# Edits to the hand-written order of an attention and MLP kernel: group 6's transposes, group 9's load, a part of each weight matrix, and two copies moved to VectorE

## The chip, the cores and the metric

The kernel runs on one core of a Trainium2 chip. The metric is the device time of one execution in microseconds (us). It is given as the median of several runs. One execution more was recorded by the hardware profiler, and all durations and instants below come from that one, counted from the start of its span.

Five engines work side by side, each through its own list of instructions in order: TensorE (PE, matmuls), VectorE (DVE), ScalarE (ACT), GpSimd (POOL) and SyncE (SP). Semaphores hold an instruction back until what it reads is there and what it overwrites is no longer needed. An instruction that waits holds back everything behind it on its engine.

## What is computed

Eight batches of twelve attention heads (448 positions, head size 64) with normalized queries and keys, and behind it an MLP over all 3584 tokens.

```python
def rmsnorm(x, g):
    rms = np.sqrt(np.mean(x * x, axis=-1, keepdims=True) + 1e-06)
    return x / rms * g
q_n, k_n = (rmsnorm(q, g_q), rmsnorm(k, g_k))
scores = scale * np.matmul(q_n, k_n.transpose(0, 1, 3, 2))
attn = softmax(scores)
x = np.matmul(attn, v)        # then heads side by side: 3584 x 768
...
h = x @ w_in                  # 768 x 2048
g = np.maximum(h, 0.0) + alpha * np.minimum(h, 0.0)
return (g @ w_out)            # 2048 x 768, float32
```

## The kernel before

**Groups.** The twelve heads of a batch are done in three groups of four, so there are 24 groups y = 0 to 23; groups 0, 1, 2 are batch 0. For each group and each of q and k the steps are, in this order:

- `load_qk` (L97): two DMAs on SP's queue for q and two for k, into one of six `nat` buffers, which are three groups' worth. A buffer is free again when the group's scaling has read it.
- `square` (L141): on ScalarE for groups 0 and 1, on POOL for the others. `reduce` (L151): the sum over the head's 64 values, on VectorE. `root` (L159): two small ScalarE instructions that give 1 over the root mean square.
- `scale` (L168): the multiplication by that, to 16 bits, mostly on POOL; group 3's q is scaled on VectorE, its k on POOL.
- Turning: positions have to go to the free dimension. Up to group 5 this is 14 transposes on PE, and two VectorE copies out of PSUM (`turn`, L188). From group 6 on (`TD` = 6) it is two DMA transposes issued on SP (`turn_dma`, L178), which wait for the scaling, and later one VectorE multiplication of kT by the gain (`turn`, L191).
- `score` and `soft` (L225, L243): seven tiles per group; PE's matmuls, then ScalarE's exp. `den`, `log`, `invert`, `attv` (L269 to L312): the sum over keys, its reciprocal and the product with v, which leave `xT`.

**MLP.** `up(b, ft)` (L344) does one of 16 column blocks of w_in for batch b: six matmuls into a PSUM bank (`hT`), ScalarE's copy `ah` = alpha times h (L354), and VectorE's maximum of the two into `gT` (L355). `down(b0, t, oh)` (L357) multiplies 128 tokens with one half (oh) of w_out's columns, 16 matmuls, eviction by VectorE (L377), output by SP's queue. Of PSUM's banks, two (tag "mm") serve ups, downs and early transposes in turn, and a pair (tag "acc") serves denominators, products with v, and now and then a spare up (`hTa`) or down (`opa`). Batch 0's first four ups are begun early (`begin`, L335): ups 0 and 1 in the "mm" banks, 2 and 3 together in the "acc" pair, named `hTb`.

**Weights.** w_in is loaded in four parts of four column blocks (`load_w_in`, L119, three DMAs each), w_out in four quarters (`load_w_out`, L131): quarters 0 and 1 are the upper and lower half of the rows for oh 0, quarters 2 ("the third") and 3 ("the fourth") the same for oh 1. The issues stand on POOL's queue, among POOL's squares and scales.

**Order.** Everything is laid out in 69 bursts n. A planner (L402 to L562) spreads the score tiles over bursts and puts ups and downs into each burst's gap. Dictionaries hang the other steps on bursts: `prep` (start of a burst, by `at`), `post` (its end, by `after`), `roots` (root and the two scales of a group, just ahead of the gap, or in `late`, after so many ups of the gap), `jobs` (a reduce after each up, or a down's own list ahead of its eviction) and `turns`. `lead` is burst 10, in which batch 0's attention ends and its ups begin; there a reduce waits until `done` is at least 4, and root and scale come when `done` is 4.

The bursts around the change, with the start of their first score matmuls in the profile:

| burst | from, us | gap | hung on it |
|---|---|---|---|
| 5 | | | second part of w_in (post) |
| 7 | 27.6 | | root and scale 3; squares 4, third part of w_in (post) |
| 8 | 30.0 | | squares 5, fourth part (post) |
| 9 | 34.5 | | load 6 (prep); reduces 4 (post) |
| 10 (`lead`) | 37.3 | ups 0 to 4 | root and scale 4; reduces 5; w_out quarters 0 and 1, squares 6 (post) |
| 11 | 45.3 | ups 5, 6 | root and scale 5 |
| 12 | 50.1 | ups 7, 8 | turn 4; load 7, v of batch 1 (prep); quarter 2 (post) |
| 13 | 53.7 | ups 9 to 11 | reduces 6 |
| 14 | 58.1 | ups 12, 13 | root, scale and DMA transposes of 6; squares 7, quarter 3 (post) |
| 15 | 61.6 | ups 14, 15 | turn 5; load 8 (prep) |
| 16 | 65.3 | down (t 0, oh 0) | load 9 (prep); reduces 7 |
| 17 | 68.9 | down (1, 0) | root, scale, DMA transposes of 7; turn 6; squares 8 (post) |
| 18 | 73.9 | down (2, 0) | squares 9 (post) |
| 19 | 80.6 | down (0, 1) | load 10 (prep); reduces 8; turn 7 |
| 20 | 87.8 | down (1, 1) | v of batch 2 (prep); root, scale, DMA transposes of 8; reduces 9 |
| 21 | 92.5 | batch 1, ups 0 to 3 | root, scale, DMA transposes of 9 |
| 22 to 24 | 97.7 | ups 4 to 15 | turn 8 in burst 23 |

Down (0, 1) of burst 19 is the first reader of w_out's quarters 2 and 3: its first eight matmuls read quarter 2, its last eight quarter 3.

Of the kernel before, what the change touches and what calls it, by code (L numbers as in the profile page):

```python
# [12 lines left out]
ALU = mybir.AluOpType  # L13
# [8 lines left out]
def kernel(  # L22
# [12 lines left out]
    nc = tc.nc  # L35

    B, H, S, D = q.shape
# [4 lines left out]
    G = HH // 2  # L42
# [6 lines left out]
    TD = min(6, NG)  # L49
# [34 lines left out]
    alpha_sb = cols[:, :NF]  # L84
# [3 lines left out]
    gT = cst.tile([128, NF, W], FP16, name="gT", tag="gT")  # L88
# [226 lines left out]
    def bank(name, spare):  # L315
        if spare:
            t = psa.tile([128, 2, 512], FP32, name=name + "a", tag="acc")
            return t[:, 0]
        return psf.tile([128, 512], FP32, name=name, tag="mm")
# [3 lines left out]
    def up_part(hT, b, ft, lo, hi):  # L323

        for i in range(lo, hi):
            for g in range(2):
                nc.tensor.matmul(  # L327
                    out=hT[:, :S],
                    lhsT=w_in_sb[:, g * G + i, ts(ft, 128)],
                    rhs=xT[b][:, g, i, :],  # L330
                    start=(i == 0 and g == 0),
                    stop=(i == G - 1 and g == 1),
                )

    def begin(ft):  # L335
# [5 lines left out]
            begun[2], begun[3] = t[:, 0], t[:, 1]  # L341
        up_part(begun[ft], 0, ft, 0, G - 1)

    def up(b, ft, spare=False):  # L344
        if b == 0 and ft in begun:
            hT = begun[ft]

            for n in {2: (2, 3), 3: ()}.get(ft, (ft,)):
                up_part(begun[n], 0, n, G - 1, G)
        else:  # L350
            hT = bank("hT", spare)
            up_part(hT, b, ft, 0, G)
        ah = ffn.tile([128, S], FP16, name="ah", tag="ah", bufs=3)
        nc.scalar.activation(out=ah, in_=hT[:, :S], func=AF.Copy, scale=alpha_sb[:, ft : ft + 1])  # L354
        nc.vector.tensor_max(out=gT[:, ft, ds((b & 1) * S, S)], in0=hT[:, :S], in1=ah)  # L355

    def down(b0, t, oh, jobs=(), spare=False):  # L357

# [44 lines left out]
    den_at, av_at, split = {}, {}, {}  # L403
# [5 lines left out]
    while m < NG * J or steps:  # L409
        n = len(bursts)  # L410
        while steps:
# [14 lines left out]
        late = both or n in dens and n in avs or any(  # L426
            y >= G for y in dens.get(n, avs.get(n, ()))
        )
        limit = 2 + late + (both and avs[n][0] >= G)
        bursts.append([])  # L430
        while len(bursts[n]) < limit and m < NG * J:
            y, j = divmod(m, J)
# [11 lines left out]
    prep, post, roots = {}, {}, {}  # L444

    def at(n, f, *a):
        prep.setdefault(max(int(n), 0), []).append((f, a))

    def after(n, f, *a):
        post.setdefault(max(int(n), 0), []).append((f, a))  # L450

    turn_at = {
        y: max(n for n in range(first_in[y]) if y >= TD or n not in dens)
        for y in range(1, NG)
    }
    turn_at[2], turn_at[G] = 5, av_at[0]
    turn_at.update((y, den_at[y - 2]) for y in range(TD, NG) if y % G == 1)
    turns = {n: y for y, n in turn_at.items()}
    jobs = {}
    for y in range(G, NG):  # L460

        early = y < G + 2
        if early:
            n = turn_at[y - 1] + 1
        elif y == G + 2:
            n = den_at[G - 1]
        elif y == 2 * G:
            n = turn_at[y] - 4
        elif y % G == 1:
            n = den_at[y - 4] - 1  # L470
        elif y % G:
            n = den_at[y - G]
        else:
            n = av_at[y - 4]
        at(n - (6 if early else 4 if y <= 3 * G else 5), load_qk, y)
        for nm in "qk":
            if y != 2 * G:
                after(n - 2, square, y, nm)
            if early:
                after(n, reduce, y, nm)  # L480
            else:
                jobs.setdefault(n, []).append((reduce, (y, nm)))
        roots[n + 1] = y
    for b in range(1, B):
        at(av_at[G * b] - 6, load_v, b)

# [26 lines left out]
    first = av_at[G - 1]  # L513
# [54 lines left out]
    for n, g in enumerate((g_q, g_k)):  # L568
        for h in range(2):
            nc.gpsimd.dma_start(  # L570
                out=rows[NF + n : NF + n + 1, ds(64 * h, 64)], in_=g.unsqueeze(0)
# [13 lines left out]
    for nm in "qk":  # L585
# [3 lines left out]
        out=gain, in0=cols[:, NF : NF + 1], in1=cols[:, NF + 1 : NF + 2]  # L589
# [12 lines left out]
    after(0, load_w_in, 0)  # L602
    for nm in "qk":
        after(2, reduce, 2, nm)
    after(5, load_w_in, 1)
    after(7, load_w_in, 2)
    after(8, load_w_in, 3)
    for c in range(4):
        after(first + (0, 0, 2, 4)[c], load_w_out, c)
    for nm in "qk":  # L610
        after(first, square, 2 * G, nm)
    roots[3] = 2
# [2 lines left out]
    for n in range(NB):  # L615
        for f, a in prep.get(n, ()):
            f(*a)
        tiles = bursts[n]

        lead = n == den_at[G - 1]  # L620
        first_tiles = tiles[: 2 if lead else split.get(n, 2)]
        for t in first_tiles:
            score(*t)
            if n == den_at[G - 1] - 1 and t == tiles[-1]:
                begin(0)
                begin(1)
            elif lead and t == tiles[0]:
                soft(*t)
                den(dens[n])
                attv(avs[n], 0, True, (log, invert))  # L630
            elif lead and t == tiles[1]:
                begin(2)
        plain = lead or n not in dens and n not in avs
        wait = plain and not lead and gaps[n] and gaps[n][0][0] is up
        if lead:
            begin(3)
        for t in tiles[:1] if wait else tiles[1:2] if lead else first_tiles:
            soft(*t)
        if n in dens and not lead:
            den(dens[n])  # L640
        if n in avs and not lead:

            for half in (1, 0) if avs[n] == (0, 1) else (0,):
                attv(avs[n], half)
        for t in () if lead else tiles[len(first_tiles) : 3]:
            score(*t)
            soft(*t)
        if n in avs and len(avs[n]) == 2 and avs[n] != (0, 1):
            attv(avs[n], 1)
        for t in () if lead else tiles[max(len(first_tiles), 3) :]:  # L650
            score(*t)
            soft(*t)
        late = []
        if wait:
            late = [(1, soft, t) for t in tiles[1:]]
        if n in roots:
            y = roots[n]
            work = [(root, (y,)), (scale, (y, "q")), (scale, (y, "k"))]
            if lead:

                late = [(2, score, tiles[2]), (2, soft, tiles[2])]
            if lead or wait and y < TD:
                late += [(4 if lead else 1, f, a) for f, a in work]
            else:
                for f, a in work:
                    f(*a)
            if y >= TD:
                turn_dma(y)
        if n in dens and not lead:
            log(dens[n])  # L670
            if gaps[n] and gaps[n][0][0] is down:
                invert(dens[n])
            else:
                late = [(1, invert, (dens[n],))]
        done = 0

        spare_at, clock = [], 0.0
        taken = n + 1 in dens or n + 1 in avs or turns.get(n + 1, TD) < TD
        for k, (f, a) in enumerate(gaps[n]):
            free = 2.3 if n in dens else (0.1, 1.2, 0.0)[len(avs.get(n, ()))]  # L680
            since += 1
            if clock >= free and not turns.get(n, TD) < TD and (
                since > 2 and not (taken and k == len(gaps[n]) - 1) or free == 0.0 and k == 0
            ):
                spare_at.append(k)
                since = 0
            clock += DOWN if f is down else UP
        ups_first = gaps[n] and gaps[n][0][0] is up
        if ups_first and n in dens and not lead:
            for f, a in jobs.pop(n, ()):  # L690
                f(*a)
        turned = n in turns and gaps[n] and (turns[n] >= TD or turns[n] < 2 * G)
        if turned and not ups_first and turns[n] >= TD:
            jobs.setdefault(n, []).append((turn, (turns[n],)))
        elif turned:
            turn(turns[n])
        for k, (f, a) in enumerate(gaps[n]):
            spare = k in spare_at
            if f is down:
                down(*a, jobs.pop(n, ()), spare)  # L700
            else:
                f(*a, spare)
                done += 1
                if n in jobs and not (lead and done < 4):
                    g, c = jobs[n].pop(0)
                    g(*c)
                    if not jobs[n]:
                        del jobs[n]
                while late and done == late[0][0]:
                    _, g, c = late.pop(0)  # L710
                    g(*c)
        if not gaps[n] and n in turns:
            turn(turns[n])
        for _, g, c in late:
            g(*c)
        if n < den_at[G - 1] - 1 and plain and n not in turns:
            spin(1)
        for f, a in jobs.pop(n, []) + post.get(n, []):
            f(*a)
# [32 lines left out]
```

## Time and profile before

| | us |
|---|---|
| median of 4 runs | 434.56 |
| runs | 433.25, 432.44, 435.87, 437.07 |
| profiled execution | 433.82 |
| its span | 432.0 |

| engine | busy, us | share of the span | instructions |
|---|---|---|---|
| PE | 416.9 | 97% | 4964 |
| ACT | 278.7 | 65% | 385 |
| DVE | 203.4 | 47% | 304 |
| POOL | 175.3 | 41% | 133 |

In the row of the page that cuts the span into 40 slices, PE's lowest digits (7, 8) stand in the first eight slices, that is before 86 us; from there on each but the last is at 9. The DMA row is at 8 or 9 in the first ten slices, and later varies. DMA transposes and loads of q, k and outputs run on SP's hardware queue (q1), v and the weights on POOL's software queue (q0). Median times from issue to landing over the whole span are 5.1 us for a half of q, 6.5 for one of k, 7.1 for v, 7.2 for a piece of w_in and 12.6 for a quarter of w_out.

How to read the lines that follow: in the timeline, a line gives start, duration, engine, source line, operation, what it writes and reads, the shapes, and in brackets the idle time ahead of it with the instruction that ended that. The chain of waits goes back from the last instruction to what released it, and so on. In a table of stretches the columns are the stretch, its length, the busy time of PE, of PE's weight loads, of DVE, ACT and POOL (in brackets the number of instructions), the granted clock, the DMA share and GB/s. A line of waits gives who waited for whom, the total, how often, and the longest.

### The profile page before, as it was taken

What the parts mean: (1) busy time and instruction counts of PE and PEld (TensorE: products, weight loads), DVE (VectorE), ACT (ScalarE), POOL (GpSimd) and SP (SyncE); (2) the same over time, 40 slices, a digit from 0 to 9 for tenths busy, and PEclk for the clock granted to TensorE, in tenths of its full rate; (3) what the DMA queues carried; (4) which work ended last, traced back from release to release, by engine and by line L of the source; (5) the groups of instructions that cost most, each with busy time, mean ns of one, the idle gap of its engine ahead of it and who ended that gap; (6) DMA issues with size and microseconds to landing.
All of it is one profiled execution on the core that took longest, in us unless ns stands there. A gap on an engine that the chain in (4) does not pass through costs nothing.

```text
span 432.0 us, 11487 instructions
## 1 busy us (share of the span) xinstructions
PE 416.9 (97%) x4964; PEld 216.2 (50%) x4964; DVE 203.4 (47%) x304; ACT 278.7 (65%) x385; POOL 175.3 (41%) x133
## 2 busy tenths in 40 slices
PE   8789899899999999999999999999999999999996
PEld 3344344454455445544555445554555445555554
DVE  3755764455545463545444463545453353233421
ACT  4998888667976677757667577757757577132300
POOL 4799796394194407380283506371163000000000
PEclk9999999999999999999999999999999999999999
DMA  8999899999568734788059743774073300211133
GB/s 191 232 231 219 155 212 149 250 187 214 118 109 193 169 92 76 156 147 186 20 96 197 165 122 62 150 150 117 20 119 86 77 1 21 56 38 32 25 73 75
DMA packets 70387, 53.85 MB, mean 125 GB/s; under 512 B 37424, under 2 KB 70336, under 8 KB 70336
## 3 DMA queue, kind: packets, MB, share of 16 engines
q1 hardware_dynamic: 55536, 40.19, 42.8%
q0 software_dynamic: 13984, 11.81, 18.9%
q10 hardware_dynamic: 816, 1.11, 1.1%
q8 instruction: 39, 0.64, 0.6%
q14 instruction: 12, 0.10, 0.1%
HBM read 45.62 MB, written 11.01 MB: 131 GB/s over the span
## 4 chain that ended last, share of the span: by engine, by line
PE 83%; DMA 6%; ACT 5%; DVE 4%; POOL 1%; issue 1%; SPq 0%; ACTq 0%
PE op L365 27%; PE hT L327 21%; PE hTa L327 11%; PE sc L232 7%; PE opa L365 6%; PE av L261 4%; DMA w_out_sb<-in_moe_w_out_dram 4%; PE dn L261 4%; ACT expT L246 3%; PE avb L261 2%; DMA nat<-in_k_dram 1%; DVE ss L154 1%; PE tps L206 1%; DVE gT L355 1%; DVE osb L377 1%; POOL sq L148 1%
## 5 line engine op out<-in xcount | busy, mean ns | idle before, releaser
L246 ACT ACTIVATE expT<-sc,expb 128x896 f16<-128x896 f32 x168 | 161.4, 1003 | 37.1 <-PE sc L232 36.1
L171 POOL TENSOR_TENSOR qs<-nat,rr 128x896 f16<-128x896 f32 x44 | 76.7, 1762 | 150.0 <-issue 79.0
L365 PE MATMUL op<-w_out_sb,gT 128*128 128x384 f16 (+1 forms) x752 | 126.5, 323 | 2.0 <-DMA w_out_sb<-in_moe_w_out_dram 2.0
L365 PEld LDWEIGHTS <-gT 128*128 128x128 f16 x912 | 85.7, 98 | 66.9 <-issue 14.4
L327 PEld LDWEIGHTS <-w_in_sb 128*128 128x128 f16 x768 | 73.1, 98 | 75.4 <-issue 11.0
L327 PE MATMUL hT<-xT,w_in_sb 128*128 128x448 f16 x510 | 107.1, 353 | 2.4 <-DVE gT L355 2.2
L354 ACT ACTIVATE ah<-hT,cols 128x448 f16<-128x448 f32 x85 | 53.7, 633 | 44.9 <-PE hT L327 44.9
L355 DVE TENSOR_TENSOR gT<-hT,ah 128x448 f16<-128x448 f32 x85 | 52.8, 623 | 51.9 <-ACT ah L354 51.9
L148 POOL TENSOR_TENSOR sq<-nat 128x896 f32<-128x896 f32 x44 | 72.9, 1677 | 7.9 <-DMA nat<-in_q_dram 3.4
L377 DVE COPY osb<-op 128x384 f32<-128x384 f32 (+1 forms) x47 | 25.8, 548 | 87.6 <-PE op L365 87.6
L232 PE MATMUL sc<-qT,kT 64*32 64x448 f16 (+1 forms) x1092 | 53.2, 356 | 4.3 <-ACT expT L246 2.8
L154 DVE TENSOR_REDUCE ss<-sq 128x14 f32<-128x896 f32 x48 | 50.5, 1077 | 9.7 <-ACT sq L146 6.2
L327 PE MATMUL hTa<-xT,w_in_sb 128*128 128x448 f16 x246 | 53.2, 352 | 0.0
L354 ACT ACTIVATE ah<-hTa,cols 128x448 f16<-128x448 f32 x41 | 26.0, 633 | 31.4 <-PE hTa L327 31.4
L355 DVE TENSOR_TENSOR gT<-hTa,ah 128x448 f16<-128x448 f32 x41 | 25.6, 623 | 26.0 <-ACT ah L354 26.0
L232 PEld LDWEIGHTS <-kT 64*32 64x32 f16 (+1 forms) x1092 | 15.0, 93 | 36.2 <-issue 30.4
L365 PE MATMUL opa<-w_out_sb,gT 128*128 128x384 f16 x160 | 27.7, 326 | 0.0
L312 DVE TENSOR_TENSOR xT<-av,rden 128x896 f16<-128x896 f32 x16 | 17.5, 1091 | 17.5 <-PE av L261 14.2
L261 PEld LDWEIGHTS <-vt 64*32 64x32 f16 (+1 forms) x1260 | 18.9, 94 | 13.2 <-issue 2.2
L261 PE MATMUL dn<-expT,ones 64*32 64x448 f16 (+1 forms) x812 | 24.2, 350 | 0.9
L261 PE MATMUL av<-expT,vt 64*32 64x448 f16 (+1 forms) x812 | 24.1, 349 | 0.0
L278 ACT ACTIVATE rden<-dn 128x896 f32<-128x896 f32 x16 | 14.5, 907 | 7.3 <-PE dn L261 7.3
(45 smaller groups left out, 160.4 us busy)
## 6 DMA issues: line engine op xcount, KB each, us to landing
out_dram<-osb SPq DMA_DIRECT2D x109, 96.0 KB, 2.3
nat<-in_q_dram SPq DMA_DIRECT2D x46, 224.0 KB, 5.1
nat<-in_k_dram SPq DMA_DIRECT2D x46, 224.0 KB, 6.5
vt<-in_v_dram POOLq DMA_DIRECT2D x16, 336.0 KB, 7.1
w_in_sb<-in_moe_w_in_dram POOLq DMA_DIRECT2D x12, 256.0 KB, 7.2
w_out_sb<-in_moe_w_out_dram POOLq DMA_DIRECT2D x4, 768.0 KB, 12.6
nat<-in_q_dram ACTq DMA_DIRECT2D x2, 224.0 KB, 5.0
nat<-in_k_dram ACTq DMA_DIRECT2D x2, 224.0 KB, 6.8
```

What stands on the lines that cost most here:

```text
L148: nc.gpsimd.tensor_mul(out=sqf, in0=src, in1=src)
L154: nc.vector.tensor_reduce(out=ss_t[y][:, "qk".index(nm)].rearrange("p h j -> p (h j)").unsqueeze(2), in_=sqs[y, nm], axis=AXIS_X, op=ALU.add,)
L171: eng.tensor_mul(out=t.rearrange("p j h d -> p h j d"), in0=nat[y, nm], in1=rr_t[y][:, "qk".index(nm)].unsqueeze(3).broadcast_to((128, 2, ...
L232: nc.tensor.matmul(out=sc[ds(64 * g + m * c, m), par, :S].rearrange("p (j c) -> p j c", j=J), lhsT=kT[ds(64 * par, 64), j, g, ts(c, m)], r ...
L246: nc.scalar.activation(out=expT[y][:, j], in_=scs[y, j][:, :, :S], func=AF.Exp, scale=QK_SCALE, bias=expb[:, 0:1],)
L261: nc.tensor.matmul(out=accs[g][ds(m * h, m), :S], lhsT=weights(g, y, par, ts(c, m), j), rhs=expT[y][ds(64 * g, 64), j, par, :], start=(j = ...
L312: nc.vector.tensor_mul(out=x, in0=av[:, :, :S], in1=r)
L327: nc.tensor.matmul(out=hT[:, :S], lhsT=w_in_sb[:, g * G + i, ts(ft, 128)], rhs=xT[b][:, g, i, :], start=(i == 0 and g == 0), stop=(i == G ...
L354: nc.scalar.activation(out=ah, in_=hT[:, :S], func=AF.Copy, scale=alpha_sb[:, ft : ft + 1])
L355: nc.vector.tensor_max(out=gT[:, ft, ds((b & 1) * S, S)], in0=hT[:, :S], in1=ah)
L365: nc.tensor.matmul(out=ops[c][:, :PW], lhsT=gT[:, ft, ts(t, 128)], rhs=w_out_sb[:, ft, ds(oh * OH + c * PW, PW)], start=(ft == 0), stop=(f ...
L377: nc.vector.tensor_copy(out=o[:, ts(c, PW)], in_=ops[c][:, :PW])
```

## The change

- **VectorE copies.** For batch 0's ups 2 and 3 the copy `ah` is made by VectorE (`tensor_scalar`) instead of ScalarE, and their maximum into `gT` is put off (`held`) until after that of up 4.
- **Roots and reduces.** In burst 10 root and scale 4 come after two ups instead of four, and the first reduce of group 5 after five ups instead of four; the second goes to burst 11. Root and scale 5 go from burst 11 to burst 12, behind its first up.
- **Group 6.** Its reduces go from burst 13 to 12; root, scale and DMA transposes from the head of burst 14's gap to the end of burst 13's (after its third up). Its load stays in burst 9 (n is one less, the distance 3 instead of 4).
- **Third quarter of w_out.** Its issue goes from the end of burst 12 to the end of burst 13, so that POOL's scale 6 is ahead of it.
- **Second part of w_in.** From the end of burst 5 to the end of burst 7, as the first of what is there, behind scale 3.
- **Group 9.** Its load goes from the start of burst 16 to the end of burst 17; its second reduce to the end of burst 20; its root, scale and DMA transposes from burst 21 to 22.

```diff
+    held = []
+
     def up(b, ft, spare=False):
...
         ah = ffn.tile([128, S], FP16, name="ah", tag="ah", bufs=3)
+        if b == 0 and ft in (2, 3):
+
+            nc.vector.tensor_scalar(
+                out=ah, in0=hT[:, :S], scalar1=alpha_sb[:, ft : ft + 1], scalar2=None,
+                op0=ALU.mult,
+            )
+            held.append((hT, ah, ft))
+            return
         nc.scalar.activation(out=ah, in_=hT[:, :S], func=AF.Copy, scale=alpha_sb[:, ft : ft + 1])
-        nc.vector.tensor_max(out=gT[:, ft, ds((b & 1) * S, S)], in0=hT[:, :S], in1=ah)
+        for hT, ah, ft in [(hT, ah, ft)] + (held if b == 0 and ft == 4 else []):
+            nc.vector.tensor_max(out=gT[:, ft, ds((b & 1) * S, S)], in0=hT[:, :S], in1=ah)
...
+    after(den_at[0], load_w_in, 1)
...
         elif y == 2 * G:
-            n = turn_at[y] - 4
+            n = turn_at[y] - 5
...
-        at(n - (6 if early else 4 if y <= 3 * G else 5), load_qk, y)
+        if y == 3 * G:
+
+            after(den_at[G], load_qk, y)
+        else:
+            at(n - (6 if early else 3 if y == 2 * G else 4 if y < 3 * G else 5), load_qk, y)
...
-                jobs.setdefault(n, []).append((reduce, (y, nm)))
-        roots[n + 1] = y
+                jobs.setdefault(n + (y == G + 2 and nm == "k"), []).append((reduce, (y, nm)))
+        if y == 3 * G:
+            after(n, *jobs[n].pop()[:1], y, "k")
+        roots[n + 1 + (y in (G + 2, 3 * G))] = y
...
-    after(5, load_w_in, 1)
     after(7, load_w_in, 2)
     after(8, load_w_in, 3)
     for c in range(4):
-        after(first + (0, 0, 2, 4)[c], load_w_out, c)
+        after(first + (0, 0, 3, 4)[c], load_w_out, c)
...
-            if lead or wait and y < TD:
-                late += [(4 if lead else 1, f, a) for f, a in work]
+            if y == 2 * G:
+                late += [(3, f, a) for f, a in work + [(turn_dma, (y,))]]
+            elif lead or wait and y < TD:
+                late += [(2 if lead else 1, f, a) for f, a in work]
             else:
                 for f, a in work:
                     f(*a)
-            if y >= TD:
+            if y >= TD and y != 2 * G:
                 turn_dma(y)
...
-                if n in jobs and not (lead and done < 4):
+                if n in jobs and not (lead and done < 5):
```

## What the change does to the time: the prediction

> **What bounds the kernel now.** The page's busy line first, then TensorE's (PE's) own waits, then a table of stretches.
>
> ```profile
> PE 416.9 (97%) x4964; PEld 216.2 (50%) x4964; DVE 203.4 (47%) x304; ACT 278.7 (65%) x385; POOL 175.3 (41%) x133
> PE hT L327 <- DVE gT L355: 2.2, 2, 1.7
> PE op L365 <- DMA w_out_sb<-in_moe_w_out_dram: 2.0, 1, 2.0
> 40.00:50.00 10.00, 8.26 (x58) 3.42 (x50) 6.22 (x9) 8.40 (x14) 6.85 (x7) 1.00 1.00 152
> 60.00:70.00 10.00, 9.47 (x104) 4.87 (x110) 6.56 (x10) 7.71 (x12) 8.62 (x7) 1.00 1.28 200
> 80.00:90.00 10.00, 7.88 (x103) 4.13 (x101) 3.58 (x5) 6.43 (x7) 6.63 (x5) 1.00 1.18 225
> 100.00:110.00 10.00, 10.00 (x65) 4.63 (x63) 5.36 (x9) 8.14 (x13) 1.60 (x1) 1.00 0.93 204
> ```
>
> PE is busy 416.9 of 432.0 us, at a granted clock of 1.00. The idle 15.1 us are what a change of order can win, and only some lie where this one works: 1.74 us in 40 to 50, 0.53 in 60 to 70, 2.12 in 80 to 90. The two waits above are nearly all of that. The timeline shows the first.
>
> ```profile
> 45.99 0.63 ACT L354 ACTIVATE ah<-hTb,cols 128x448 f16<-128x448 f32 x1 [0.69 <-DVE gT L355]
> 47.17 3.33 POOL L171 TENSOR_TENSOR qs<-nat,rr 128x896 f16<-128x896 f32 x2 [3.15 <-ACT rr L166]
> 48.19 0.61 DVE L355 TENSOR_TENSOR gT<-hT,ah 128x448 f16<-128x448 f32 x1
> 48.86 1.29 PE L327 MATMUL hT<-xT,w_in_sb 128*128 128x448 f16 x6 [1.74 <-DVE gT L355]
> 60.35 1.29 PE L327 MATMUL hT<-xT,w_in_sb 128*128 128x448 f16 x6 [0.42 <-DVE gT L355]
> ```
>
> Up 6 (48.86) needs the bank of up 4, freed by its gT (48.19 to 48.80). That gT was late because ACT did the copies of ups 2 and 3 and group 4's root before it. Up 13 at 60.35 has the same wait, 0.42 us. The second place, from the chain of waits and the timeline:
>
> ```profile
> 67.67 18.69 DMA w_out_sb<-in_moe_w_out_dram
> 82.96 1.47 PE L365 MATMUL op<-w_out_sb,gT 128*128 128x384 f16 x8
> 86.41 1.46 PE L365 MATMUL op<-w_out_sb,gT 128*128 128x384 f16 x8 [1.98 <-DMA w_out_sb<-in_moe_w_out_dram]
> ```
>
> The waiting matmuls are the last eight of down (0, oh 1): they read w_out's fourth quarter, which GpSimd (POOL) issued at 67.67 and which landed at 86.36. PE was ready at 84.43.
>
> **VectorE (DVE) copies and the earlier root.** From ACT go two copies of 0.63 us (L354's mean), out of the stretch before up 4's copy; root 4 (0.31 + 0.23) comes before them instead of after. ACT then runs: copies 0 and 1 until 43.88, exp until 44.78, root 4 until 45.35, and copy 4 when up 4's matmuls end (45.37) until 46.0. DVE has no row of this operation; the gT rows of the same 448 columns out of PSUM (0.62) bound it above, the eviction of 384 columns (0.55) below; I take 0.62, the same size. DVE: gT1 ends 44.54, two copies to 45.78, gT4 46.03 to 46.65, gT2 and gT3 to 47.9. Up 4's bank is free 2.15 us earlier, before PE wants it (47.1), so the 1.74 us go. hTb's banks are held until 47.9; their next user, group 4's transposes, comes at 49.
>
> What is late next is DVE, with 1.24 us more and group 6's reduces one burst earlier: reduce 5q to 49.0, gT5 49.6, reduce 5k 50.7, gT6 51.3; up 8 wants that bank at 51.15. Group 4's transposed copies (0.62 + 0.68) end at 52.6 where score (4, 0) wants them at 52.5, gT7 53.2 where up 9 wants its bank at 53.0. Reduce 6q waits for a square that ends at 53.1 by the POOL sum below, reduce 6k for one at 54.7; gT8 and gT9 are queued behind them (54.9, 56.6), and up 12 would start at 57.3 instead of 58.63. Lead there 1.33; with reduces 6 gone from burst 13, up 13's 0.42 goes too: **lead 1.75**. Bounds: 2.16 with DVE hidden throughout, 0.4 if each of these near misses costs half a microsecond.
>
> **The second w_in load.** It has three POOL issues (1.46 + 0.71). Before, they ran from 28.55 to 30.7, in time in which POOL only waited for root 3 (ready 30.48). Moved behind scale (3, k), they push POOL's later work by 2.2 us, and win scale (3, k) at most the 0.27 between 30.48 and 30.75. I take nothing: that scale lasted 2.40 us instead of 1.68 beside a VectorE scale that ran until 31.60, and ended 1.55 us after it, as at 22.74 (VectorE until 23.78, POOL until 25.32). The Trainium skill ("SBUF — State Buffer", the rule on the shared port pair) says that a VectorE operation with two SBUF inputs locks out a GpSimd one until it ends; by it the gain is exactly nil, by the start times 0.27, and the transposes behind it began on VectorE's xT anyway (33.45).
>
> So POOL: the load 33.2 to 35.3, squares 4 to 38.6, third load to 40.8, squares 5 to 44.05, fourth to 46.2. The second part of w_in is first read at 44.07; its last issue at 34.6 plus 5.1 to 8.9 us to landing gives 39.7 to 43.5. Hidden, with 0.6 us to spare at worst, and each microsecond over would be paid in full. Scale 4 runs from 46.2 to 49.55 instead of 47.17 to 50.50, since root 4 is ready at 45.35.
>
> **Group 6 ahead of the third quarter.** POOL continues: two w_out quarters to 51.4, squares 6 to 54.7, v to 56.05, scale 5 to 59.4 (before 58.84; its transposes come at 60.4), scale 6 to 62.75 (before 64.4), third quarter to 63.7 (before 61.1), squares 7 to 67.0, fourth quarter issued at 67.0 (before 67.67). The third quarter took 13.1 us to land and is needed at 82.96 less the lead, 81.2: hidden by some five microseconds. SP issues group 6's DMA transposes at 61.1 and 62.8 (before 62.86 and 64.50). That is needed: kT6 landed at 76.05, VectorE waited 1.56 us for it, and PE's score (6, 0) at 77.58 would now come at 75.8. With 11.6 us to landing, 74.4. Hidden, else up to 1.3.
>
> **Group 9's load behind it.** It leaves SP's place at 71.45 to 76.7 and goes behind group 7's transposes and the outputs of burst 17. The transposes, before at 81.97 and 83.31 because SP stood in nat 9, come at about 72.6 and 74.5. The queues' rows for 76 to 78 us show what loads cost the w_out quarter (POOL's queue q0, SP's q1; packets, MB, share):
>
> ```profile
> q1 hardware_dynamic: 213, 0.35, 68.0%
> q0 software_dynamic: 210, 0.16, 51.5%
> ```
>
> One quarter is 0.79 MB, and 0.69 MB of q0 moved from 74 to 86. Without nat 9 (0.92 MB at 0.20 to 0.25 MB per us, 3.7 to 4.6 us) the quarter lands at 86.36 - 0.67 - 4.1 = 81.6, before the 82.7 where PE wants it. With group 7's transposes in its way (group 6's took from 66 to 74 some 4.6 us of all engines: 20, 37, 121 and 82% of two microseconds each) it lands at 86.2. I take the middle, 84, because their data begin to move 4 to 5 us after the issue, at 77 or later, when most of the quarter is through. PE then ends its wait 86.36 - 84.0 = **2.4 us** earlier, which holds all of the lead: what lies before an unlanded quarter is not added to it.
>
> A rule on this: the Trainium skill ("DMA: Bandwidth & Descriptors", Queues, rings and completion order) has each engine take the queues in turn, one packet each. The row above agrees (213 to 210); 70 to 72 us, with q1 528 and q0 97 under transposes, does not. By the rule a quarter of 1024 packets waits for at most 1024 transpose packets, some 1.5 us at 1509 per 2 us, lands near 83.1, and the gain is 3.3.
>
> **After that.** From 90 us PE has no waits, so the lead stays unless group 8 is late. kT8 is read at 104.13 and would be wanted at 101.7; three more ups can run before a bank is missing (3.4 us). Squares 9 end at about 90.5 (before 89.63), group 8's scale and transposes follow 0.4 later. VectorE's reduce 9q may wait a microsecond in burst 20, ahead of an eviction; the next gT comes at 92.6, and reduce 9k ends by 91.6. I take 0, at worst 0.6.
>
> **Sum.** The profiled execution took 433.82 us, 1.82 around the span of 432.0; 433.82 - 2.4 = 431.4. The median of the four runs (432.44 to 437.07) is 0.74 higher: 434.56 - 2.4 = **432.2 us**. About 1%, 4.3 us, is what a measurement tells from no change.
>
> **The rivals.**
> All waits go: the quarter lands by 82.7, both DVE stalls vanish, and small waits with them (0.1 in 80 to 90, 0.24 in 50 to 60). 1.74 + 0.42 + 1.98 + 0.34 = 4.5, 430.1. For it: nat 9 alone is worth 4.1 us to the quarter. Against: DVE's near misses and the transposes. Chance 0.17.
> The stall only moves: transposes 7 take nat 9's place and the quarter still lands near 86.2, so the lead is waited away; 434.4 (432.9 to 436). For it: the DMA engines are busy in every slice from 50 to 90. Chance 0.19.
> Slower: nat 9 too late. Issued near 80.3 behind transposes whose k issue took 3.9 to 4.3 us, with the longest landing of that stretch, 14.1, it lands at 94.4; square 9k ends 96.1, v and scale 8 follow (1.5 + 3.3) to 100.9, kT8 lands 8 later, 108.9, against 101.7. Less the 3.4 of ups, PE loses 3.8, and VectorE in burst 20 stands some 5 more: with 2.4 gained, 434.56 + 6.4 = 441. It decides from squares 9 ending 3.4 us after 90.5; against it is the median landing, 8.8, with fewer transfers around. Chance 0.11.
> The forecast, 432.2 with its own range 430.4 to 433.8, has 0.53.
>
> **Numbers.** Faster by over 1% (below 430.2): half of the first rival, which lies on that bound, and the forecast's lower tail, 0.09 + 0.06. Slower by over 1% (above 438.9): most of the third, 0.10. Within: 0.75. The range goes from 429.3 (first rival with the runs' spread) to 436.0 (the end of the second); outside lie the third rival and some of the first's lower end.
>
> **What would show it.** Up 6 following up 5 with no DVE wait, and up 8, 9 and 12 without one: the first step. Fourth quarter issued near 67, transposes 7 near 73, and PE's wait on w_out near 1.3 us (0 is the first rival, 3.5 the second): the second step. Lead at 100 us of 2.4. Wrong: a wait of PE on w_in at 44, kT6 or kT8 as a releaser of DVE ahead of waiting gT, or POOL's square 9 waiting past 88.

## The result, and the profile after

| | before | changed |
|---|---|---|
| median of executions | 432.99 us (60) | 435.89 us (41) |
| lowest to highest | 430.89 to 437.80 | 432.46 to 439.96 |
| profiled execution | 433.82 | 436.11 |
| its span | 432.0 | 434.2 |

The changed kernel takes 1.0055 times as long, 95% interval 1.0040 to 1.0071: 2.4 us slower (2.9 by the two medians). The forecast was 2.4 us faster. This ratio and those below leave out executions more than 1.5% above the fastest of the same kernel, of the changed kernel one of 41. The two profiled spans differ by 2.2 us; two later records of the changed kernel have spans of 432.5 and 432.0, so the one read here is the slowest of three.

The page of the changed kernel, its busy line first, then PE's waits that are new or have moved (total, times, longest):

```profile
PE 417.0 (96%) x4964; PEld 216.3 (50%) x4964; DVE 205.1 (47%) x306; ACT 277.7 (64%) x383; POOL 175.7 (40%) x133
PE sc L232 <- DVE kT L192: 2.2, 1, 2.2
PE op L376 <- DMA w_out_sb<-in_moe_w_out_dram: 1.9, 1, 1.9
PE hT L327 <- DMA w_in_sb<-in_moe_w_in_dram: 0.8, 1, 0.8
PE opa L376 <- DVE xT L312: 0.6, 1, 0.6
PE hT L327 <- DVE gT L366: 0.4, 1, 0.4
```

PE's work is the same (417.0 for 416.9). The 2.2 us of waits on VectorE's gT are down to 0.4, which is what the first step promised, and the 1.98 us on the w_out quarter stand as before. New are 0.8 us on w_in and 2.2 + 0.6 us behind kT6. The table of stretches says the same: 1.74 us of idle PE from 40 to 50 have become 0.97, none from 70 to 80 has become 2.80.

```profile
40.00:50.00 10.00, 9.03 (x67) 3.94 (x64) 6.87 (x11) 7.76 (x13) 9.96 (x9) 1.00 1.20 208
70.00:80.00 10.00, 7.20 (x151) 3.58 (x148) 2.43 (x4) 6.88 (x10) 3.33 (x2) 1.00 1.22 187
80.00:90.00 10.00, 7.93 (x83) 4.34 (x85) 3.70 (x6) 4.84 (x7) 3.36 (x2) 1.00 1.37 147
```

The same stretch before, and kT6 (group 6's kT) before, from its issue to VectorE's multiplication, which waits for its landing:

```profile
70.00:80.00 10.00, 10.00 (x201) 5.03 (x186) 3.17 (x5) 8.16 (x11) 3.74 (x3) 1.00 1.39 171
64.50 3.67 SPq L181 DMA_TRANSPOSE kT<-qs  x1
76.09 0.45 DVE L192 TENSOR_SCALAR kT<-kT,gain 128x896 f16<-128x896 f16 x1 [1.56 <-DMA kT<-qs]
```

The timeline of the changed kernel gives the places, in order of time:

```profile
45.31 0.55 PE L327 MATMUL hT<-xT,w_in_sb 128*128 128x448 f16 x2 [0.80 <-DMA w_in_sb<-in_moe_w_in_dram]
62.55 3.31 SPq L181 DMA_TRANSPOSE kT<-qs  x1
66.70 0.94 POOL L133 DMA_DIRECT2D w_out_sb<-in_moe_w_out_dram  x1
78.13 0.45 DVE L192 TENSOR_SCALAR kT<-kT,gain 128x896 f16<-128x896 f16 x1 [4.80 <-DMA kT<-qs]
78.64 0.38 PE L232 MATMUL sc<-qT,kT 64*64 64x448 f16 x4 [2.19 <-DVE kT L192]
88.08 1.46 PE L376 MATMUL op<-w_out_sb,gT 128*128 128x384 f16 x8 [1.92 <-DMA w_out_sb<-in_moe_w_out_dram]
93.35 1.68 POOL L148 TENSOR_TENSOR sq<-nat 128x896 f32<-128x896 f32 x1 [8.72 <-DMA nat<-in_q_dram]
```

A ledger by instants of the two timelines: the first down starts at 64.99 for 66.19, a lead of 1.20 us. Score (6, 0) starts at 78.64 for 77.58, 1.06 behind. The eight matmuls on the fourth quarter start at 88.08 for 86.41, 1.67 behind; the first up of burst 22 at 100.43 for 98.17, 2.26 behind, after the 0.42 us at 98.70; and so it stays to the end, where this execution's span is 2.2 us longer. So the copies and the earlier root won what they were to win, and the transfers lost more: kT6, issued 1.95 us earlier than before, landed 2.0 us later (15.6 us to landing for 11.6), and the fourth quarter, issued 0.97 us earlier, landed near 88.0 for 86.36.

One more number is needed to understand the medians: 28 of the 41 executions of the changed kernel have a mean granted clock of 0.996 or less (of the kernel before about one in ten in the runs below), where the three recorded ones have 0.999 to 1.000. The other 13 have a median of 434.57 us, the 28 one of 436.36. So the ledger tells of an execution at full clock, and none at the lower mean clock was recorded of this kernel.

### The profile page after: what moved, and what is told of

Read it like the earlier page. It is cut to its first block, busy times and chain, and to the rows that moved or that the text cites. A ratio compares the mean times of both kernels' runs of the same rounds, so it can differ in the third digit from the quotient of the medians.

```text
span 434.2 us, 11492 instructions
## 1 busy us (share of the span) xinstructions
PE 417.0 (96%) x4964; PEld 216.3 (50%) x4964; DVE 205.1 (47%) x306; ACT 277.7 (64%) x383; POOL 175.7 (40%) x133
## 4 chain that ended last, share of the span: by engine, by line
PE 79%; DMA 9%; DVE 3%; POOL 3%; ACT 3%; issue 2%; SPq 1%; POOLq 0%; ACTq 0%
PE op L376 26%; PE hT L327 20%; PE hTa L327 10%; PE sc L232 7%; PE opa L376 6%; PE dn L261 4%; PE av L261 4%; DMA kT<-qs 4%; DMA nat<-in_k_dram 3%; DMA w_in_sb<-in_moe_w_in_dram 2%; ACT expT L246 2%; PE avb L261 2%; POOL qs L171 2%; DVE ss L154 1%; DVE osb L388 1%
```

## The experiments

V stands for the two VectorE copies, R for the moved roots and reduces of groups 4 and 5, W for the second w_in load, S for group 6's early turn, Q for the third quarter, N for group 9's edits. The changed kernel is V R W S Q N. Ratios are to the kernel before, run on the same chip.

**One edit undone at a time, and the first two alone.** The first run undoes W:

```diff
-    after(den_at[0], load_w_in, 1)
+    after(5, load_w_in, 1)
```

> The changed kernel with the second w_in load alone back at the end of burst 5. Theory (collisions: DMA transposes and the w_out quarters slow each other): only the 0.8 us wait of up 4 on w_in goes; kT6 still lands 14 us or more after its issue, PE still waits for it and for the fourth quarter; the time is 0 to 1 us under the changed kernel's, so +0.3 to +0.5% on before. Rival (backlog: with the load moved, the DMA engines idle from 32 to 34 us and all later transfers are late): kT6 lands by 75, the fourth quarter by 85.5, and the time is 0 to 0.5% under before.

Measured: 0.9984 (0.9945 to 1.0023); the recorded execution has a span of 429.3, 2.7 under before and 4.9 under the changed kernel. The rival holds, by the ratio: kT6 had landed by 72.4, 5.7 us before the changed kernel's, though its issue came only 1.35 us earlier, and the fourth quarter at 83.75. That is the prediction nearly to the letter (74.4, 84, and a span of 432.0 - 2.4 = 429.6).

```profile
61.20 1.71 SPq L181 DMA_TRANSPOSE kT<-qs  x1
72.42 1.85 DVE L192 TENSOR_SCALAR kT<-kT,gain 128x896 f16<-128x896 f16 x1
83.76 1.46 PE L376 MATMUL op<-w_out_sb,gT 128*128 128x384 f16 x8 [1.54 <-DMA w_out_sb<-in_moe_w_out_dram]
```

Where the time went shows in one stretch, 30 to 38 us, in which the load moved before and didn't after (last column GB/s). In order: before, changed, and this run.

```profile
30.00:38.00 8.00, 7.69 (x178) 3.91 (x174) 6.44 (x8) 7.04 (x11) 7.98 (x8) 1.00 1.16 232
```
```profile
30.00:38.00 8.00, 7.88 (x182) 4.17 (x186) 5.54 (x7) 7.41 (x10) 7.49 (x6) 1.00 0.63 122
```
```profile
30.00:38.00 8.00, 7.88 (x182) 4.11 (x182) 6.44 (x8) 7.41 (x10) 7.98 (x7) 1.00 1.14 229
```

110 GB/s less over 8 us are 0.9 MB. Part of it is made up by 50 us, where the engines had gaps before; at 62, when group 6's transposes are issued, the changed kernel has moved 6.63 MB since 28 (12 us at 164 GB/s, 10 at 208, 12 at 215) and this run 7.17 (236, 184 and 208). The 0.54 MB are 2.6 us at the 0.205 MB per us of that stretch. With the 1.35 us of the issue they would be 4.0 of the 5.7 us. That is an estimate, and it isn't shown that the backlog made kT6 late: two others without W, below, have kT6 at 77.4 and 77.0. And the timed executions of this kernel spread from 429.79 to 439.60, with a mean clock from 1.000 down to 0.991. Three of the twelve (436.98, 437.15, 439.60) are not in the ratio; with them the mean, 434.14, is 0.1% over before, and the step from the changed kernel is no longer clear of the noise. The order is fast when all lands in time, and not robust.

The second run undoes N (load 9 at the start of burst 16, its reduce and root as before):

```diff
-        if y == 3 * G:
-            after(den_at[G], load_qk, y)
-        else:
-            at(n - (...), load_qk, y)
+        at(n - (...), load_qk, y)
```

> The changed kernel with group 9's edits alone undone (load at the start of burst 16, second reduce and root as before). Theory (moving the load let group 7's transposes meet the fourth quarter): transposes 7 go back behind nat 9, the quarter lands at 85 to 86.5 in place of 88.0, POOL's square 9 no longer waits 8.7 us; the time falls by 1 to 2 us, to before's or 0.2% either way. kT6 stays late (about 78), as its transposes and the third quarter stand where they did. Rival (nat 9's load was worth its place): the quarter lands later than 88, and the time is 0.8 to 1.5% over before.

Measured: 1.0145 (1.0113 to 1.0176). My theory of that moment falls, the rival holds: the quarter landed near 90.5, and moving load 9 away was worth 0.9% of the changed kernel's time. The record shows something new too.

```profile
90.51 2.72 PE L376 MATMUL op<-w_out_sb,gT 128*128 128x384 f16 x8 [4.40 <-DMA w_out_sb<-in_moe_w_out_dram]
```
```profile
88.00:89.00 1.00, 0.00 (x0) 0.00 (x0) 0.00 (x0) 0.00 (x0) 0.68 (x1) 1.00 0.69 62
89.00:90.00 1.00, 0.00 (x0) 0.00 (x0) 0.00 (x0) 0.00 (x0) 1.00 (x2) 0.52 1.12 71
91.00:92.00 1.00, 1.00 (x4) 0.46 (x3) 0.00 (x0) 0.00 (x0) 0.30 (x1) 0.50 1.11 333
95.00:96.00 1.00, 1.00 (x16) 0.52 (x12) 0.00 (x0) 0.70 (x1) 0.00 (x0) 0.57 1.18 250
96.00:97.00 1.00, 1.00 (x16) 0.44 (x9) 0.51 (x1) 0.39 (x1) 0.00 (x0) 1.00 1.16 268
```

Third from last is the granted clock. PE stood from 86.1; at 89.0, 2.9 us into the wait, the clock went to 0.5, and it came back at 95.9. Eight matmuls took 2.72 us in place of 1.46. A wait of 4.4 us thus cost about 7: from these eight matmuls to the next down 5.97 us passed in place of 3.41, some 2.6 us more. The Trainium skill ("TensorE: Matmul & The Clock Gate", Part 1) gives a window of about 3.4 us, idle for the clock to fall and busy for it to return; here it fell a little earlier, after 2.9, and returned later, some 5.4 us after work began.

The third run undoes Q, `(0, 0, 3, 4)` to `(0, 0, 2, 4)`:

> The changed kernel with the third quarter of w_out alone back at the end of burst 12, ahead of scale 6 on POOL. Theory (group 6's transposes were slowed by the quarter issued with them): kT6 lands by 75.5 and PE's 2.2 us wait on it goes; the third quarter lands by 75 in place of 82; what is gained is partly waited away at the fourth quarter, if that still lands near 87: 0.5 to 1.5 us under the changed kernel. Rival (transposes take 12 to 15 us with any q0 traffic): kT6 lands at 77 or later again, the scale behind the quarter's issue moving the transposes by 0.9, and the time is that of the changed kernel.

Measured: 0.9996 (0.9969 to 1.0023), 0.59% under the changed kernel, 2.5 us, with all twelve executions in the ratio; more than expected, and by the other transfer. kT6 still landed late (77.3, PE waited 1.5 us), as the rival had it; but the fourth quarter was there in time. The sixteen matmuls run through, and no wait on w_out is left:

```profile
83.92 2.77 PE L376 MATMUL op<-w_out_sb,gT 128*128 128x384 f16 x16
```

The fourth run has V and R alone on the kernel before:

> The kernel before with the two VectorE copies and the moved roots and reduces of groups 4 and 5 alone. All theories: up 6's 1.74 us wait goes, PE is 1.5 to 1.9 us ahead from 49 to 74 us. Theory (what lies before an unlanded transfer is waited away): kT6 at about 76 costs 0.3 to 0.8 of it, and the fourth quarter at 86.4 the rest: the time is within 0.2% of before. Rival (the lead frees buffers earlier, so transfers land earlier): 0.3 to 0.5% faster.

Measured: 1.0004 (0.9985 to 1.0022). The first down starts at 64.47, a lead of 1.72 us; PE then waits 1.0 + 0.6 us behind kT6, of which 0.6 us of lead are left at score (6, 0), and 0.9 on the quarter. The quarter landed 1.0 us earlier than before, and the recorded span ends 1.0 us ahead; the timed executions are level. By the timed executions, then, the lead is waited away in front of transfers that have not landed, as the first theory has it; in the recorded one 1.0 of its 1.72 us is left.

**Pairs, and single edits.** Q and W both undone (V R S N):

> The changed kernel with both the second w_in load and the third quarter of w_out back at their old places. Theory (backlog: each of the two pushes work off idle DMA engines, and kT6 and the w_out quarters pay): kT6 lands by 73, the fourth quarter by 82, PE has no wait over 1 us between 46 and 100; span 427.5 to 429.5, time 0.6 to 1.1% under before, with little spread. Rival (the two edits do not add, and what one wins the other gives back): within 0.2% of before, as each alone was.

Measured: 0.9986 (0.9969 to 1.0003). A miss: neither the expected gain nor kT6 by 73. Its issue came at 63.39, as the third quarter's issue, 59.06, again stands ahead of scale 6 on POOL, and it landed after 14 us at 77.4. The quarter cost nothing. What undoing the two edits wins does not add. The four kernels that have V, R, S and N in common say it at a glance:

| | third quarter moved (Q) | at its old place |
|---|---|---|
| second w_in load moved (W) | 1.0055 | 0.9996 |
| at its old place | 0.9984 | 0.9986 |

Only both moves together cost something that the intervals show. The lower left ratio is the one that leaves out three executions.

W alone on the kernel before:

> The kernel before with the second w_in load alone moved behind group 3's scaling. Backlog theory: up 4 waits 0.5 to 1.5 us for w_in, the engines move about 100 to 150 GB/s from 30 to 38 us instead of 230, kT6 lands at 77 to 79 and the fourth quarter at 88 or later: 0.5 to 1.2% slower than before. Rival (the load's place only matters for up 4, all later lateness being the other edits'): at most 0.3% slower, kT6 at 76 to 77, the quarter by 87.

Measured: 1.0022 (1.0002 to 1.0041), between the two expectations, slower, if just so, but less than the backlog theory asked: 0.7 us of wait on w_in, kT6 at 78.1 (1.5 us of PE), the quarter at 87.1. The traffic from 30 to 38 us is 122 GB/s as in the changed kernel. By 62 us 6.62 MB have moved since 28, for 6.88 before: 0.26 MB or 1.3 us of backlog, half of what W makes with the other edits around it. So W is a small loss on its own, and beside Q a larger one (0.7% by the ratio of the first run).

N alone on the kernel before:

> The kernel before with group 9's edits alone. Theory (nat 9 out of the way lets the fourth quarter land earlier): the quarter lands at 82 to 85, PE's 2.0 us wait on it goes or shrinks below 1; up 6's 1.74 us stay; 0.2 to 0.5% faster than before. Rival (group 7's transposes take its place): the quarter lands at 86 or later, within 0.2% of before or slower.

Measured: 0.9979 (0.9964 to 0.9995): faster, as the theory says, if just so. Its mechanism isn't shown: the recorded execution is the slowest of twelve (span 432.3, the others 429.4 to 430.6), and in it the quarter landed at 86.2 as the rival has it, with 1.1 us of wait. V, R and N:

> The kernel before with the VectorE copies, the moved roots and reduces of groups 4 and 5 and group 9's edits; group 6, the third quarter and w_in as before. Theory: kT6 lands at 75 to 76.5 and costs PE 0.5 to 1.5 us at burst 18, the fourth quarter lands by 84 and costs nothing: 0.3 to 0.6% faster than before. Against the kernel with group 6 early as well it shows what turning group 6 early is worth: 0.3 to 0.5%.

Measured: 0.9982 (0.9964 to 1.0001), less than expected, and not faster for certain; the mechanism is there (no wait on the quarter, 1.3 us behind kT6). It is level with V R S N, so turning group 6 early by DMA (S) is worth nothing that can be measured here.

**The clock, and the two quarters together.** Two more records of the changed kernel were to catch one of its executions at 0.996 or less:

> The changed kernel once more, for a second recorded execution. Theory (the lower mean clock in 28 of its 41 runs, 0.996 or less, comes from a PE stall of about 3 us or more, after which the clock is halved for some 5 us): in an execution at 0.996 or less, a stretch behind the wait on kT6 or on the fourth quarter stands at 0.5, that wait is 3 us or longer, and eight matmuls behind it take 2.7 us in place of 1.5. Rival (a lower clock spread over the whole span): all stretches slightly under 1.00.

> As the run before it: a third recorded execution of the changed kernel, since one in three has the full clock and then shows nothing of this.

Inconclusive: both have a clock of 1.000, spans of 432.5 and 432.0, waits of 0.8 and 0.7 us for kT6's scores and 2.0 and 1.8 on the quarter. They do show how far the landing of kT6 varies with one and the same order: 78.1, 76.6 and 76.2. That the lower clocks of the changed kernel come from longer waits of this kind stays an inference from two records of other kernels with 4.4 us, the one above and the next. Those have 6.8 us at 0.5 and a mean clock of 0.991; a mean of 0.996 over 434 us would be some 3.5 us at 0.5, about half of that (an estimate).

The landing of kT6 can be followed through all thirteen records in which group 6 is turned by DMA. It was issued between 61.2 and 64.6 us, and in twelve of them it landed between 76.1 and 78.1, 11.6 to 15.6 us later: an earlier issue bought no earlier landing. The thirteenth is the first run's 72.4.

Then W undone, and the fourth quarter issued right behind the third, `(0, 0, 3, 4)` to `(0, 0, 3, 3)`:

> The kernel e1_w_in_back with the fourth quarter issued right behind the third, at the end of burst 13, ahead of POOL's squares 7 (3.3 us earlier). Theory (that kernel's only wait was 1.5 us on the fourth quarter, and its runs at a clock of 0.996 or less come from the same wait being longer): the quarter lands 1 to 3 us earlier, nothing stands, 0.5 to 0.9% faster than before with few runs at a lower clock. Rival (the quarter's place in the queue doesn't decide, the engines are full): lands as before, within 0.2% of before, spread as wide; or kT6 comes later than 75 and PE waits there instead.

Measured: 0.9989 (0.9949 to 1.0028), spread from 429.68 to 439.93: the rival. Six of the twelve are too far above the fastest to be in the ratio; the mean of all twelve is 0.5% over before. One execution has the lowest span of all, 427.9, and the recorded one 437.5, with kT6 at 77.0, a wait of 4.4 us on the quarter and the clock at 0.5 behind it. Its table of stretches shows what the engines did while group 6's transposes were in flight:

```profile
68.00:70.00 2.00, 2.00 (x50) 0.96 (x35) 0.09 (x1) 1.96 (x3) 0.00 (x0) 1.00 1.69 27
70.00:72.00 2.00, 2.00 (x16) 1.10 (x18) 0.02 (x1) 1.94 (x5) 1.11 (x1) 1.00 1.47 74
```

A DMA share of 1.69, and 27 GB/s. The engines were not full of bytes; they were held up. The same hole lies in every kernel so far, at whatever place the transposes have beside a quarter, if not of the same depth (116 GB/s in its lowest 2 us with Q undone): 105 to 131 GB/s from 70 to 76 us before, 77 to 127 from 66 to 72 in the changed kernel and 84 to 153 once more from 82 to 90, where group 7's transposes, no longer held back by nat 9, met the late fourth quarter. Before, that second hole was 2 us long (108 GB/s from 86 to 88); the quarter had landed at 86.36. The queues' rows of the kernel before show transposes in company, 70 to 72 us, and group 7's with no quarter left, 88 to 90:

```profile
q1 hardware_dynamic: 528, 0.13, 120.6%
q0 software_dynamic: 97, 0.06, 23.9%
```
```profile
q1 hardware_dynamic: 1509, 0.57, 115.9%
```

With the quarter landed and the hole over, q1 moved nearly three times the packets, most of them still transposes' (1350 of 1509 under 512 B), at 283 GB/s. So the transposes are not slow by themselves.

**The transposes taken away.** Group 6 turned on PE, as groups 0 to 5 are, on the kernel before and with nothing else changed in the program (the third line only makes the branch include group 6):

```diff
-    TD = min(6, NG)
+    TD = min(7, NG)
-            n = turn_at[y] - 4
+            n = turn_at[y] - 3
-        turned = n in turns and gaps[n] and (turns[n] >= TD or turns[n] < 2 * G)
+        turned = n in turns and gaps[n] and (turns[n] >= TD or turns[n] < TD)
```

> The kernel before with group 6 turned by 14 transposes on PE and two VectorE copies, as groups 0 to 5 are, in place of two DMA transposes; nothing else changed. Theory (a DMA transpose in flight beside a w_out quarter brings the engines' traffic down to 30 to 130 GB/s for some 6 us, which is what makes kT6 and the quarter late, whatever is issued first): from 66 to 78 us the engines move 190 GB/s or more, the fourth quarter lands by 83 (before 86.4), PE's 2.0 us wait goes; PE does 0.95 us more: 0.1 to 0.4% faster than before, with little spread. Rival (the engines are simply full of bytes): the stretch stays at 105 to 130 GB/s or the quarter lands at 85.5 or later, and the time is 0 to 0.3% over before.

Measured: 0.9977 (0.9953 to 1.0000), as the theory has it, with executions between 431.85 and 432.64 us. The stretch from 66 to 78 us, before and in this run:

```profile
66.00:78.00 12.00, 12.00 (x233) 5.87 (x230) 5.47 (x8) 9.96 (x13) 5.95 (x5) 1.00 1.39 165
```
```profile
66.00:78.00 12.00, 12.00 (x238) 6.05 (x235) 5.83 (x9) 9.29 (x12) 8.03 (x7) 1.00 1.24 236
```

A lower share, and 71 GB/s more: what held the engines up is gone from this stretch, and down (0, 1) runs through with no wait on w_out. The quarter landed at 83.4, 15.3 us after its issue at 68.08, a little later than the theory asked. Something else moved along: SP's queue no longer stood in the transposes, so loads 8 and 9 were issued from 56.7 and 63.2 us on, before from 68.2 and 71.5. The hole in the traffic goes with the transposes; how much of the quarter's earlier landing is due to the loads, no run separates.

```profile
83.06 2.77 PE L365 MATMUL op<-w_out_sb,gT 128*128 128x384 f16 x16
```

The same with V, R and N:

> The kernel e8_no_group6 (VectorE copies, moved roots and reduces, group 9's edits) with group 6 turned on PE. Theory: no wait on kT6, the fourth quarter lands by 81 where PE wants it at 82, up 6's 1.74 us gone too: 0.6 to 1.0% faster than before. Rival (group 7's DMA transposes, now the only ones beside the quarter, hold it up as much): quarter at 84 or later, 0 to 0.3% faster.

Measured: 0.9948 (0.9924 to 0.9971), **faster than both kernels**, at a median of 430.96 with executions from 430.44 to 431.35, under 1 us apart where those of the changed kernel are 7.5 apart. It is a little under the 0.6 to 1.0% expected, which the interval reaches. Group 7's transposes dug the same hole (75 and 58 GB/s from 76 to 80), but PE waited for nothing in it: the quarter had landed at 79.8. And with group 7 on PE too (`TD` = 8):

> As the run before it, with group 7 turned on PE too (0.95 us of PE more). Theory: the quarter lands as early or earlier, so 0.2% slower than with group 6 alone on PE, unless group 7's transposes beside the quarter cost over 1 us there; little spread. Rival: 0.3% faster than it, since nat 9 also lands earlier and squares 9 no longer wait.

Measured: 0.9995 (0.9974 to 1.0015), 0.5% slower than with group 6 alone: its transposes cost 0.95 us of PE, and they wait 1.1 us for VectorE's xT, which the expectation did not have. The quarter lands in time either way.

## Why the prediction was wrong

- **What bounds the kernel.** Right: PE was bound by two waits, and both are places where the changed kernel differs.
- **VectorE copies and the earlier root.** Right in mechanism and size. Copies took 0.63 us (0.62 predicted), up 6's 1.74 us went, gT4 came at 46.56 in the changed kernel and 45.82 in V R alone (46.03 predicted). The lead was 1.72 us in V R alone (1.75 predicted), 1.20 in the changed kernel, where PE waited 0.8 us for w_in.
- **The landings: the step that failed.** The prediction shifted each transfer's landing with its issue: kT6 11.6 us behind it, "74.4, hidden", and the fourth quarter at 84, from which the whole gain of 2.4 us was taken. In the record kT6 took 15.6 us and landed at 78.1, and the quarter landed at 88.0; PE's last eight matmuls of down (0, 1) started 1.67 us later than before, not 2.4 earlier. In the two other records of the changed kernel it is 76.6 and 76.2, 86.6 and 85.9. The quarter came last, so its landing sets the loss of this record (PE was ready for it at 86.16). The fall of the engines' traffic while transposes and a quarter are in flight together had no term at kT6, and at the quarter one of which the prediction took half.
- **The second w_in load.** It was costed at nothing, "hidden, with 0.6 us to spare at worst". On its own it costs 0.2%; beside the moved quarter it turns 0.9984 into 1.0055. The part landed at 45.2, later than the bound of 43.5, and PE waited 0.8 us; that its data met those of group 6's load (issued 33.06 to 36.3) is a likely reason that no run tests. And the prediction looked at POOL, but not at the DMA engines behind it: the load had filled 30 to 36 us, which stood half empty without it, and 0.54 MB were left over for the stretch in which the prediction itself had every slice busy. That scale (3, k) would win nothing was right: it ended at 33.03, 1.55 us after VectorE's, as the rows had it.
- **Group 6 ahead of the third quarter.** Issue times were right to 0.3 us (kT6 62.55 for 62.8, third quarter 62.47 for 62.75, fourth 66.70 for 67.0). What the order buys was wrong: kT6 was issued 1.95 us earlier and landed 2.0 us later. Undoing Q gains 0.59% beside W, and nothing without it.
- **Group 9's load.** Right in sign, since undoing it costs 0.9% and it wins 0.2% alone. Its size came from a sum of bytes over a rate, 0.92 MB at 0.20 to 0.25 MB per us, and the runs show a rate that falls to half of that and less while transposes are in flight beside it. The quarter landed at 88.0, not 84, past the 86.2 that was the upper bound. That bound was itself a little low: the four shares it quotes for group 6's transposes add up to 5.2 us of all engines, not 4.6, which gives 86.8. Packets in turn (the rule weighed there) would have said 83.1, which the changed kernel's three records, 85.9 to 88.0, do not bear out.
- **After that.** Taken as 0, "at worst 0.6"; it came to 0.6 (2.26 behind at 100 us for 1.67 at 88). Squares 9 ended at 97.0, not 90.5, POOL waiting 8.7 us for nat 9, and PE paid 0.42 us through VectorE's gT at 98.70. The third rival named that chain; it came, but cost about a tenth of its 6.4 us, as kT8 was read without a wait.
- **The rivals.** The second came nearest: group 7's transposes did take nat 9's place and the lead was waited away. The measured 435.89 even lies in its range, 432.9 to 436, but by luck: that range counts from a median of 434.56 in four executions, and sixty have 432.99. Counted from before, it reached 1.4 us slower, and the runs show 2.4. The prediction had no rival in which moving work earlier makes the transfers themselves slower.

Settled: the loss needs W and Q together, and undoing Q takes it away for certain; N is a small gain, and V with R does no harm. Turning group 6 on PE takes away the wait for kT6, the wait for the quarter and the spread (twelve executions within 1 us), and with V, R and N it brings a gain. Open: how much of that is the missing transposes and how much the earlier loads of groups 8 and 9, why the two kinds of transfer slow each other, by what path W adds to it (the backlog is argued, not shown), and, for want of a record, that the lower clocks of 28 executions come from waits of about 3 us or more.

## What to carry to other kernels

A load that lies in time in which its engine only waits may be the one that keeps the DMA engines busy: before moving it, look at the traffic of the stretch that it leaves, not only at its deadline. A transfer's landing time is no constant to be shifted with its issue; where transposes and weight loads overlap, take one of them off the DMA engines, even for a microsecond of PE, and the spread goes with the mean (group 6's paid for that here, group 7's did not). And before a lead is counted, find the next transfer that has not landed: the lead ends there.

## What the runs showed of the hardware

- Group 6's DMA transposes in flight beside a quarter of w_out brought the DMA engines' traffic from some 200 GB/s down to between 27 and 121 GB/s in the lowest 2 us of each of the thirteen records, and below 145 GB/s for 6 us or more in ten. With them off the DMA engines the 12 us from 66 to 78 moved 236 GB/s for 165. A shorter hole, 8 to 143 GB/s from 103.0 to 104.5 us in the changed kernel, stood with group 8's transposes in flight and no quarter.
- In both records with a wait of 4.4 us PE's granted clock fell to 0.5 after 2.9 us without work and was back at 1.00 6.8 us later, so that the wait cost about 2.5 us beyond itself, while waits of 2.2 us left it at 1.00.
- One and the same order landed kT6 at 76.2, 76.6 and 78.1 us, and the fourth quarter at 85.9, 86.6 and 88.0.
